# Layer 2 of an attention and two-layer feed-forward kernel: two passes of four slice pairs for three passes, smaller token blocks, another order of products

## The chip, the cores and the metric

One core of one Trainium2 chip runs the whole program: TensorE (PE) for matrix products, VectorE (DVE), ScalarE (ACT) and GpSimd (POOL) for elementwise work, SyncE (SP) as the queue that issues every DMA. The metric is device time in microseconds. The kernel before takes 1144.64 us (median of 3 runs, 1144.38 to 1147.03).

## What is computed

```python
attn_out = attention(q, k, v, tau)           # 4 batches x 8 heads x 576 x 64, thresholded softmax
x  = attn_out as (2304 tokens, 512)
h  = x @ w_in                                # layer 1: 512 -> 2048 -> 512
g  = where(h >= 1, h, where(h <= -1, 0, (h + 1) ** 2 / 4))
x  = g @ w_out
h2 = x @ w_in2                               # layer 2: 512 -> 2048 -> 512
out = (s * relu(h2) ** 2 + b) @ w_out2
```

The weights come as 64-bit floats and are converted on the chip. Every operand of a product is split in a high and a low part (a cast, and a subtraction that leaves the rest), and a product is three matmuls: high x high, high x low, low x high.

## The kernel before

Three stages follow each other: attention, with a part of layer 1 beside it (to about 440 us), the rest of layer 1 (to 702 us), and layer 2 (to the end).

**A planner sets the order.** The code records tasks with `add(alternatives, priority, reads, writes)`. An alternative is an engine with a time that the planner takes it to need. `Sched.run` then plays a list schedule and emits all instructions in that order, one fixed sequence for each engine. Where a task has several alternatives, `best` takes the engine that would end first; for tasks recorded before the point `sch.soft` a third of DVE's speed is assumed (`PENALTY`), later ones see its plain time. Banks of PSUM are taken by `Group`: the first free of the eight. Banks 0 and 1 are the two halves of one tile (`ps2_0` in the program), banks 2 and 3 of another (`ps2_1`), banks 4 to 7 are tiles of their own.

**Layer 1, late part.** `hidden` makes a tile of h (12 matmuls of 256 or 320 columns), which passes DVE, ACT, DVE, ACT, and a subtraction (`both_sub`, line 954, by DVE or POOL). `l1_out` multiplies it by w_out, three tiles behind (`LEAD`). `load_parts` brings a token block of x to a staging buffer by DMA and copies it into place with 4 x 2 copies (lines 916 to 918). Beside this the weights of layer 2 are prepared (`weight_set`, `half_rows`, `store`): loaded as 64-bit words, converted by one ACT and four DVE steps, combined, split, and put in place for the first pass, or stored to DRAM (`wD`) for later ones.

**Layer 2.** The 16 slices of 128 hidden units are worked off in passes, `PASSES = (3, 3, 2)` pairs of slices, so each pass goes over all tokens in three blocks of 768: nine steps. A step is `gemm1`, then `gemm2`.

- `gemm1` computes a 2 x 2 block product with seven products instead of eight. For each product p in `ORDER` the x operand is made (up to two subtractions, line 1190, and a split, line 1191) into one of three buffers of a ring, and each of the `nj` pairs of slices then takes six matmuls (line 1207) of 384 columns. Products 1, 6, 7, 4 add up in one bank of each pair (`A`), 5 and 3 in another (`Bk`), 2 in one of its own. After each product the bank is copied (`copied`, line 1141) or added (`joined`, line 1145) to a row in SBUF, before the next product of that bank may write it.
- When both halves of a row are there, `activated` runs relu (ACT line 1162 or POOL line 1163), square (ACT line 1164), scale and bias (DVE line 1165 or POOL line 1166), and the split into `G`.
- `gemm2` multiplies the rows of G with w_out2 (line 1239): for each row, for each 128 tokens, three matmuls of 512 columns into one bank per 128 tokens. In the first pass the sums go to DRAM (`yD`), in later ones the earlier sums are read back and joined.

All units of weights for the next pass are stored to DRAM during one pass, with the kit of buffers `kits[1]`, and fetched into place as the last step of that pass frees the places.

Of the kernel before, what the change touches and what calls it, by code (L numbers as in the profile page):

```python
# [362 lines left out]
def attention_then_ffn(tc, qk, v, tau, w1, w2, s2, b2, out):  # L363
# [62 lines left out]
    wD = dp.tile([11 * sum(PASSES[1:]), 128, 512], F32, name="wd")  # L426
# [389 lines left out]
    def final():  # L816
        late["cm"].__exit__(None, None, None)
        xg.__exit__(None, None, None)
        late["cm"] = tc.tile_pool(name="final", bufs=1, side="right")
        q = late["cm"].__enter__()  # L820
        arena["PR"] = q.tile([128, PR_BYTES // 4], F32R, name="pr")
        arena["PF"] = q.tile([128, PF_BYTES // 4], F32, name="pf")
# [80 lines left out]
    xp_b, yp_b = [Buf("LG", O_XP + 5120 * i, 4 * TM) for i in range(2)], Buf("LG", 0, 4 * TM)  # L903

    def load_parts(q, xs):
# [3 lines left out]
        for x, t in enumerate((XH, XL)):  # L909
            add([("sp", DMA_ISSUE, lambda x=x: nc.sync.dma_start(out=xp_b[x](0, 4 * T).rearrange("p (k t) -> p k t", k=4),  # L910
                                                          in_=xT[x, :, t0:t0 + T].rearrange("(k p) t -> p k t", p=128)))],
                pr, r=["late"] + [("xT", q, p, x) for p in range(H // 2)], w=xp_b[x].keys(0, 4 * T), lag=128 * 16 * T)
            for j in range(4):
                c = slice(j * T, j * T + T)
                k = ("XH", "XL")[x]
                add([("act", act_ns(T), lambda c=c, t=t, x=x: nc.scalar.copy(out=t[xs][:, c], in_=xp_b[x](c.start, T))),
                     ("pool", pfast_ns(T), lambda c=c, t=t, x=x: nc.gpsimd.tensor_copy(out=t[xs][:, c], in_=xp_b[x](c.start, T))),
                     ("dve", fast_ns(T), lambda c=c, t=t, x=x: nc.vector.tensor_copy(out=t[xs][:, c], in_=xp_b[x](c.start, T)), True)],
                    pr, r=xp_b[x].keys(j * T, T), w=[(k, xs, j)])
# [141 lines left out]
    class Pass:  # L1061

        def __init__(self, n, f0, nj, first, slots):
            self.n, self.f0, self.nj, self.first = n, f0, nj, first
            self.unit = [Buf(*places[i], 512, F32R) for i in slots[:11 * nj]]

        def product(self, p, j):
            return ORDER.index(p) * self.nj + j
# [4 lines left out]
        def rows(self):  # L1073
            return [2 * j + 1 for j in range(self.nj)] + [2 * j for j in range(self.nj)]

        def store(self, kit, n, val, kv, to, prio):

            u = [o_b[turn("o", NO)] if self.n else self.unit[i] for i in to]
# [334 lines left out]
```

## Time and profile before

| what | us |
|---|---|
| median of 3 runs | 1144.64 |
| the profiled execution | 1146.08 |
| its span (first to last instruction) | 1144.2 |
| attention and the part of layer 1 beside it | 0 to 440 |
| layer 1, the rest | 440 to 701.9 |
| layer 2, pass 1 (3 pairs) | 701.9 to 858.5 |
| layer 2, pass 2 (3 pairs) | 858.5 to 1012.7 |
| layer 2, pass 3 (2 pairs) and the last output | 1012.7 to 1144.2 |

A row of the trace gives the time that an engine was busy in a stretch, or one group of instructions (line, engine, operation, what it writes and reads), or what ended the idle time before an instruction. Matmuls overlap: one of 512 columns is shown with some 0.39 us and the next starts 0.23 us later, so the spacing of the starts is what counts.

### The profile page before, as it was taken

The page shows a single profiled execution, that of the slowest core. Times are in us where ns is not written, and L with a number is a line of the kernel's source. Part 1 is how long each engine was busy: PE and PEld are TensorE (multiplying, and loading weights), DVE is VectorE, ACT ScalarE, POOL GpSimd, SP SyncE. Part 2 cuts the span into 40 slices and gives each one's busy share as a digit, 9 for nine tenths or more (in the row PEclk, how much of TensorE's full clock was granted, in tenths as well). Part 3 has the DMA queues.
Part 4 walks back from the last instruction along what each step waited for, and adds up shares of the span by engine and source line. Part 5 has one row for each costly group of instructions (what it writes and reads, how often), then busy time and mean ns, then how long its engine had stood idle before and what let it go on. Part 6 is the DMA issues. An engine that isn't in the chain of part 4 may idle for free.

```text
span 1144.2 us, 19743 instructions
## 1 busy us (share of the span) xinstructions
PE 1084.8 (95%) x6910; PEld 936.7 (82%) x6910; DVE 834.1 (73%) x1792; ACT 688.3 (60%) x1340; POOL 419.5 (37%) x600
## 2 busy tenths in 40 slices
PE   9899999999999999999999999899998999988787
PEld 6557777888988989999999999787878888767566
DVE  6999999687587755599995555879687886726454
ACT  6998889778788876455553333646545473513322
POOL 5666766787588452000210000312232220413312
PEclk9999999999999999999999999999999999999999
DMA  5546453543444311544553423273949576423321
GB/s 179 182 144 177 128 169 108 155 126 98 128 122 128 96 53 47 169 140 159 164 165 111 129 98 101 74 257 136 342 161 355 189 262 221 156 94 128 110 92 56
DMA packets 95714, 169.06 MB, mean 148 GB/s; under 512 B 9600, under 2 KB 42368, under 8 KB 95616
## 3 DMA queue, kind: packets, MB, share of 16 engines
q1 hardware_dynamic: 95616, 167.81, 45.4%
q8 instruction: 54, 0.88, 0.3%
q14 instruction: 44, 0.36, 0.1%
HBM read 120.33 MB, written 47.45 MB: 147 GB/s over the span
## 4 chain that ended last, share of the span: by engine, by line
PE 65%; DVE 18%; ACT 10%; issue 3%; DMA 1%; POOL 1%; DVEq 0%; ACTq 0%; POOLq 0%
PE ps L1239 15%; PE ps L1207 14%; PE ps L941 10%; PE ps L1017 8%; PE ps L974 6%; PE ps L728 4%; PE ps L690 3%; DVE p L634 3%; PE ps L580 3%; ACT p L669 2%; ACT e L629 2%; DVE lg L1145 2%; PE ps L571 2%; DVE stt L626 1%; ACT pt L682 1%
## 5 line engine op out<-in xcount | busy, mean ns | idle before, releaser
L1239 PE MATMUL ps<-lr,pr 128*128 128x512 f32 x756 | 178.9, 396 | 2.7 <-DVE lg L1145 1.6
L1239 PEld LDWEIGHTS ps<-lr,pr 128*128 128x128 f32 x756 | 141.2, 188 | 38.9 <-ACT lf L1164 2.1
L1207 PE MATMUL ps<-lr 128*128 128x384 f32 x720 | 138.3, 342 | 20.1 <-ACT lg L1141 9.6
L1207 PEld LDWEIGHTS ps<-lr 128*128 128x128 f32 x720 | 123.5, 188 | 34.1 <-ACT lg L1141 14.4
L941 PE MATMUL ps<-xh,lr 128*128 128x256 f32 (+1 forms) x640 | 140.0, 299 | 1.8 <-DVE lf L951 1.7
L634 DVE SCALAR_TENSOR_TENSOR p<-ps,stt,e 128x576 f32<-128x576 f32 x144 | 116.0, 812 | 27.7 <-ACT e L629 16.5
L626 DVE TENSOR_REDUCE stt<-ps 128x1 f32<-128x576 f32 x144 | 105.9, 748 | 22.5 <-PE ps L580 12.7
L949 ACT ACTIVATE lf<-lf,cst 128x320 f32<-128x320 f32 (+1 forms) x128 | 68.8, 537 | 77.4 <-DVE lf L947 76.9
L629 ACT ACTIVATE e<-ps,stt 128x576 f32<-128x576 f32 x144 | 105.8, 748 | 14.6 <-DVE stt L626 11.7
L941 PEld LDWEIGHTS ps<-xh,lr 128*128 128x128 f32 x640 | 106.3, 188 | 4.8 <-DVE lf L951 2.7
L1141 ACT COPY lg<-ps 128x384 f32<-128x384 f32 x89 | 41.2, 482 | 114.6 <-PE ps L1207 114.2
L669 ACT ACTIVATE p<-p,stt 128x576 f32<-128x576 f32 (+3 forms) x106 | 86.4, 819 | 15.7 <-DVE stt L653 14.7
L941 PE MATMUL ps<-xl,lr 128*128 128x256 f32 (+1 forms) x320 | 94.1, 294 | 0.0
L974 PE MATMUL ps<-g,lr 128*128 128x320 f32 (+1 forms) x600 | 88.3, 299 | 0.5 <-ACT lf L983 0.5
L690 PE MATMUL ps<-ident,p 128*128 128x128 f32 x576 | 82.6, 275 | 3.8 <-ACT pt L682 2.2
L682 ACT COPY pt<-ps 128x512 f32<-128x512 f32 x141 | 79.4, 588 | 7.1 <-PE ps L690 6.5
L974 PEld LDWEIGHTS ps<-g,lr 128*128 128x128 f32 x600 | 81.9, 188 | 1.4 <-ACT lf L983 0.7
L953 ACT CAST g<-lf 128x320 fp32r<-128x320 f32 (+1 forms) x128 | 55.3, 432 | 45.4 <-DVE lf L951 44.4
L690 PEld LDWEIGHTS ps<-ident,p 128*128 128x128 f32 x576 | 66.4, 140 | 17.2 <-ACT pt L682 3.0
L1017 PE MATMUL ps<-g,wh 128*128 128x320 f32 (+1 forms) x384 | 78.7, 297 | 0.8 <-DVE lf L1027 0.6
L947 DVE TENSOR_SCALAR lf<-ps 128x320 f32<-128x320 f32 (+1 forms) x128 | 57.9, 453 | 28.7 <-PE ps L941 28.3
L951 DVE TENSOR_TENSOR lf<-lf,ps 128x320 f32<-128x320 f32 (+1 forms) x128 | 57.4, 449 | 26.0 <-ACT lf L949 24.5
(121 smaller groups left out, 2459.3 us busy)
## 6 DMA issues: line engine op xcount, KB each, us to landing
wd<-pr SPq DMA_DIRECT2D x55, 256.0 KB, 4.3
lg<-y1T SPq DMA_DIRECT2D x9, 1536.0 KB, 7.5
lg<-in_w_dram SPq DMA_DIRECT2D x23, 512.0 KB, 3.9
pf<-in_w_dram SPq DMA_DIRECT2D x21, 512.0 KB, 5.3
vr<-in_v_dram SPq DMA_DIRECT2D x32, 320.0 KB, 3.5
st<-in_w_dram SPq DMA_DIRECT2D x40, 256.0 KB, 3.8
lr<-wd SPq DMA_DIRECT2D x37, 256.0 KB, 5.8
r<-in_qk_dram SPq DMA_DIRECT2D x32, 288.0 KB, 3.1
```

Of the source, the lines that this page charges most:

```text
L626: add([("dve", 665, lambda: nc.vector.tensor_reduce(out=nm[:, x:x + 1], in_=Sv(), axis=AX.XY, op=ALU.min))], at(pr, "min"), r=[kg], w=[ks[ ...
L629: add([("act", 624, lambda: nc.scalar.activation(out=ev, in_=Sv(), func=AF.Exp, bias=nm[:, x:x + 1], scale=-1.0))], at(pr, "exp"), r=[kg, ...
L634: nc.vector.scalar_tensor_tensor(out=p[:, x * S:x * S + S].rearrange("p (a c) -> p a c", a=2), in0=Sv(), scalar=nthr[:, x:x + 1], in1=ev, ...
L669: nc.scalar.activation(out=p[i:j, o:o + w], in_=p[i:j, a:a + w], func=AF.Identity, scale=rc[i:j, x:x + 1], bias=un[i:j, x:x + 1])
L682: add([("act", actp_ns(n), lambda: [nc.scalar.copy(out=a, in_=b) for a, b in zip(dst, src())]), ("dve", dve_ns(n), lambda: [nc.vector.tens ...
L690: nc.tensor.transpose(bank[g.banks[0]][:, j * 128:(j + 1) * 128], p[:, c0 + j * 128:c0 + (j + 1) * 128], ident)
L941: nc.tensor.matmul(o, a, x, start=(n == 0), stop=(n == 11))
L949: add([("act", act_ns(T, True), lambda: nc.scalar.activation(out=c, in_=c, func=AF.Square, bias=half, scale=0.5))], fp, r=[], w=kc)
L974: nc.tensor.matmul(o, a[:, c], x, start=(f == 0 and n == 0), stop=(f == nf - 1 and n == 2))
L1017: nc.tensor.matmul(o, a[:, c], x, start=(f == f0 and n == 0), stop=(f == f1 - 1 and n == 2))
L1207: nc.tensor.matmul(o, a, y, start=(i == 0 and p in (1, 5, 2)), stop=(i == 5), skip_group_check=p not in (1, 5, 2))
L1239: nc.tensor.matmul(o, a, y, start=(f == rows[0] and s == 0), stop=(f == rows[-1] and s == 2))
```

## The change

Layer 2 runs in two passes of four pairs of slices. The tokens come in four blocks (640, 640, 512, 512), so there are eight steps, and a matmul of gemm1 has 320 or 256 columns. The order of the products is 1, 5, 6, 3, 7, 2, 4: neighbours write other banks, and the even rows are complete after product 2, the odd ones after product 4; gemm2 takes the even rows first. relu is on ACT alone. Layer 1's x goes by DMA straight into place. Of the first pass's 44 units of weights 12 have no place until layer 1 is over: they are stored to DRAM and fetched (`NPLACE`, `stored`). Two weight sets of the second pass are prepared early (`EARLY`). `sch.soft` is set behind the preparation of the first pass, so that DVE's penalty holds in the whole of layer 1. The planner's times for scale and bias are raised. There are 3 output buffers for the first pass (`y_b`) and 2 store buffers in kit 1 (`NO`), where there were 4 and 3. `PAD` moves the tiles `pr` and `pf` from an address of 32 modulo 64 to one of 0.

```diff
-PASSES = (3, 3, 2)
+PASSES = (4, 4)
-BT = 768
-HT = BT // 2
-ORDER = (1, 6, 7, 4, 5, 3, 2)
+BLOCKS = ((0, 640), (640, 640), (1280, 512), (1792, 512))
+BT = 640
+ORDER = (1, 5, 6, 3, 7, 2, 4)
-NLEFT, NEXTRA = 31, 10
+NLEFT, NPLACE = 32, 44
+EARLY = 2
...
-            add([("sp", DMA_ISSUE, lambda x=x: nc.sync.dma_start(out=xp_b[x](0, 4 * T).rearrange("p (k t) -> p k t", k=4),
...
-            for j in range(4):
...
-                add([("act", act_ns(T), lambda c=c, t=t, x=x: nc.scalar.copy(out=t[xs][:, c], in_=xp_b[x](c.start, T))),
...
+            add([("sp", DMA_ISSUE, lambda x=x, t=t: nc.sync.dma_start(out=t[xs][:, 0:4 * T].bitcast(F32).rearrange("p (k t) -> p k t", k=4),
...
+            self.unit = unit[:11 * nj]
+            self.stored = [bool(n) or u.mem == "PR" for u in self.unit]
...
         def rows(self):
-            return [2 * j + 1 for j in range(self.nj)] + [2 * j for j in range(self.nj)]
+            return [2 * j for j in range(self.nj)] + [2 * j + 1 for j in range(self.nj)]
...
-        add([("act", act_ns(n), lambda: nc.scalar.activation(out=h(), in_=h(), func=AF.Relu)),
-             ("pool", pfast_ns(n), lambda: nc.gpsimd.tensor_scalar(out=h(), in0=h(), scalar1=0.0, scalar2=0.0, op0=ALU.max, op1=ALU.add))], pr, w=kh)
+        add([("act", act_ns(n), lambda: nc.scalar.activation(out=h(), in_=h(), func=AF.Relu))], pr, w=kh)
...
-        made = {6: [(T1, b12, b11), (T2, b22, T1)], 7: [(b12, b22, b12)], 4: [(T2, b21, T2)]}
+        made = {5: [(T1, b12, b11)], 6: [(T2, b22, T1)], 7: [(b12, b22, b12)], 4: [(T2, b21, T2)]}
...
-                if p == 5:
-                    activated(t, G_b[2 * j + 1], po)
-                elif p == 2:
-                    activated(t, G_b[2 * j], po)
+                if p == 2:
+                    activated(T, even, G_b[2 * j], po)
+                elif p == 4:
+                    activated(T, odd, G_b[2 * j + 1], po)
...
-    sch.soft = len(sch.tasks)
...
+    for job in passes[0].jobs() + work[:EARLY]:
+        job(kits[0])
+    sch.soft = len(sch.tasks)
+    load_x(*BLOCKS[0])
+    for i, s in enumerate(passes[0].stored):
+        if s:
+            passes[0].fetch(i, fresh()[1])
```

What PE runs in gemm1 of the last step, before: 14 products of six matmuls, all of them on the two banks of the tile `ps2_0`, most behind a wait for ACT (`Activation_49`) or DVE.

```order
L1207 MATMUL ps2_0_89<-lr_66 128x384 [waits DVE_49,Pool_49]
L1207 MATMUL ps2_0_89<-lr_66 128x384 x11
L1207 MATMUL ps2_0_89<-lr_66 128x384 [waits Activation_49]
L1207 MATMUL ps2_0_89<-lr_66 128x384 x5
L1207 MATMUL ps2_0_89<-lr_66 128x384 [waits Activation_49]
L1207 MATMUL ps2_0_89<-lr_66 128x384 x5
```

And in the second step of the change: products 1 and 5 (four pairs each) and the start of 6.

```order
L1204 MATMUL ps2_0_89<-lr_66 128x320 [waits DVE_49,Pool_49]
L1204 MATMUL ps2_0_89<-lr_66 128x320 x11
L1204 MATMUL ps2_1_90<-lr_66 128x320 [waits Activation_49]
L1204 MATMUL ps2_1_90<-lr_66 128x320 x5
L1204 MATMUL ps1_1_92<-lr_66 128x320 x6
L1204 MATMUL ps2_1_90<-lr_66 128x320 [waits DVE_49,Pool_49]
L1204 MATMUL ps2_1_90<-lr_66 128x320 x5
L1204 MATMUL ps1_0_91<-lr_66 128x320 [waits Activation_49]
L1204 MATMUL ps1_0_91<-lr_66 128x320 x5
L1204 MATMUL ps4_0_1152<-lr_66 128x320 x6
L1204 MATMUL ps4_1_1153<-lr_66 128x320 x6
L1204 MATMUL ps2_0_89<-lr_66 128x320 x12
```

Seven other products now stand between two that add to one bank; `ps2_1` holds a bank of product 1 and one of product 5.

What DVE runs in layer 1's late part, before, in its full stretch: the two steps of a hidden tile, the conversions of weights (L885, L887) and the subtractions of both (L550 into `g` and `wl`).

```order
L951 TENSOR_TENSOR lf_67<-lf_67,ps1_1_92 128x256
L947 TENSOR_SCALAR lf_67<-ps1_0_91 128x256
L885 SCALAR_TENSOR_TENSOR lg_5309<-lg_5309 128x512
L550 TENSOR_TENSOR g5_80<-lf_67,g5_80 128x256
L951 TENSOR_TENSOR lf_67<-lf_67,ps1_0_91 128x256
L887 SCALAR_TENSOR_TENSOR lg_5309<-lg_5309 128x512
L550 TENSOR_TENSOR g0_75<-lf_67,g0_75 128x256
```

What POOL runs in the change there, where layer 2's first weight sets are made:

```order
L551 TENSOR_TENSOR g3_78<-lf_67,g3_78 128x256
L551 TENSOR_TENSOR lr_66<-lg_5309,lr_66 128x256 x2
L551 TENSOR_TENSOR g4_79<-lf_67,g4_79 128x256
L551 TENSOR_TENSOR lg_5309<-lg_5309 128x256
L551 TENSOR_TENSOR lr_66<-lg_5309,lr_66 128x256
L551 TENSOR_TENSOR g5_80<-lf_67,g5_80 128x256
L551 TENSOR_TENSOR lg_5309<-lg_5309 128x256 x3
```

The subtractions of the hidden tiles and of the weight sets have moved from DVE to POOL.

## Rows read from the trace of the kernel before

**Rows 1.** The page, part 1: busy us (share) xinstructions.

```profile
PE 1084.8 (95%) x6910; PEld 936.7 (82%) x6910; DVE 834.1 (73%) x1792; ACT 688.3 (60%) x1340; POOL 419.5 (37%) x600
```

**Rows 2.** Busy by stretch: layer 1's rest (sum), pass 3, layer 2 (sum).

```profile
sum 262.00, PE 261.14 PEld 256.54 DVE 189.90 ACT 125.18 POOL 18.30; mean PE 87.05 PEld 85.51 DVE 63.30 ACT 41.73 POOL 6.10
...
1012.70:1144.20 131.50, 103.84 (x469) 82.60 (x467) 64.89 (x85) 38.87 (x58) 33.13 (x23) 1.00 0.29 99
sum 442.30, PE 397.72 PEld 333.49 DVE 291.38 ACT 195.22 POOL 110.91; mean PE 132.57 PEld 111.16 DVE 97.13 ACT 65.07 POOL 36.97
```

**Rows 3.** L1207 by step: PE busy (x), PEld, clock, DMA; sums of 6, of 3.

```profile
858.50:885.10 26.60, 23.28 (x126) 21.51 (x125) 1.00 1.01 367
...
sum 158.60, PE 141.78 PEld 128.96; mean PE 23.63 PEld 21.49
...
sum 74.70, PE 52.54 PEld 41.92; mean PE 17.51 PEld 13.97
```

**Rows 4.** L1239 by step: the last of nine, and their sum.

```profile
1122.40:1139.80 17.40, 16.97 (x72) 13.26 (x72) 1.00 0.06 22
sum 204.60, PE 202.95 PEld 160.36; mean PE 22.55 PEld 17.82
```

**Rows 5.** Timeline of PE, unbroken runs: start, us, line, columns, count.

```profile
871.92 3.97 PE L1207 MATMUL ps<-lr 128*128 128x384 f32 x22
...
885.65 23.73 PE L1239 MATMUL ps<-lr,pr 128*128 128x512 f32 x101
...
290.20 3.97 PE L974 MATMUL ps<-g,lr 128*128 128x320 f32 x26
...
207.75 3.23 PE L974 MATMUL ps<-g,lr 128*128 128x256 f32 x26
```

**Rows 6.** Timeline of PE in a step of pass 3; [idle before <- releaser].

```profile
1054.95 2.27 PE L1207 MATMUL ps<-lr 128*128 128x384 f32 x12
1057.79 1.32 PE L1207 MATMUL ps<-lr 128*128 128x384 f32 x6 [0.57 <-ACT lg L1141]
...
1078.79 1.31 PE L1207 MATMUL ps<-lr,pr 128*128 128x384 f32 x6 [0.65 <-DVE lg L1145]
```

**Rows 7.** ACT at the same place.

```profile
1057.25 0.48 ACT L1141 COPY lg<-ps 128x384 f32<-128x384 f32 x1 [7.90 <-PE ps L1207]
```

**Rows 8.** Timeline of PE in the last step of pass 2.

```profile
981.84 2.32 PE L1207 MATMUL ps<-lr 128*128 128x384 f32 x12 [0.16 <-DVE lg L1145]
984.81 1.32 PE L1207 MATMUL ps<-lr 128*128 128x384 f32 x6 [0.65 <-DVE lg L1145]
986.86 2.31 PE L1239 MATMUL ps<-lr,pr 128*128 128x512 f32 x8 [0.74 <-DVE lg L1145]
```

**Rows 9.** Groups by line, layer 2: xcount | busy us, mean ns | idle before.

```profile
L1163 POOL TENSOR_SCALAR lg<-lg 128x768 f32<-128x768 f32 x17 | 47.5, 2800 | 26.4 <-DVE lg L1145 26.3
L550 DVE TENSOR_TENSOR pr<-lg,pr 128x768 fp32r<-128x768 f32 x47 | 46.3, 985 | 8.2 <-ACT pr L844 8.2
...
L1145 DVE TENSOR_TENSOR lg<-lg,ps 128x384 f32<-128x384 f32 x72 | 38.3, 551 | 36.5 <-PE ps L1207 36.1 <-PE ps L1239 0.2
...
L1165 DVE TENSOR_SCALAR lg<-lf,cst 128x768 f32<-128x768 f32 x35 | 27.3, 779 | 1.6 <-ACT lf L1164 1.6
...
L1162 ACT ACTIVATE lg<-lg 128x768 f32<-128x768 f32 x31 | 25.5, 841 | 35.2 <-DVE lg L1145 35.2
```

**Rows 10.** Groups by line and form: POOL, whole program; DVE in layer 1.

```profile
L549 POOL TENSOR_TENSOR g<-lf,g 128x320 fp32r<-128x320 f32 x27 | 23.7, 883 | 6.4 <-ACT g L953 5.8
L549 POOL TENSOR_TENSOR g<-lf,g 128x256 fp32r<-128x256 f32 x23 | 17.2, 748 | 2.0 <-ACT g L953 1.7
...
L880 POOL TENSOR_SCALAR lg<-lg 128x512 f32<-128x512 f32 x2 | 1.4, 710 | 15.5 <-ACT lg L877 15.5
...
L887 DVE SCALAR_TENSOR_TENSOR lg<-lg 128x512 uint32<-128x512 uint32 x23 | 15.9, 693 | 0.0
```

**Rows 11.** The page, part 6: fetch of a weight unit, us to landing.

```profile
lr<-wd SPq DMA_DIRECT2D x37, 256.0 KB, 5.8
```

More of the change, by code (lines that the diff above doesn't have):

```diff
@@ L821, in final @@
         arena["PR"] = q.tile([128, PR_BYTES // 4], F32R, name="pr")
-        arena["PF"] = q.tile([128, PF_BYTES // 4], F32, name="pf")
+        arena["PF"] = q.tile([128, (PF_BYTES + PAD) // 4], F32, name="pf")
     def after(tasks, fn, key, r=()):
@@ L901, in span @@
         return q // 2 * S + q % 2 * 256, 320 if q % 2 else 256
[L903 removed]
+    yp_b = Buf("LG", 0, 4 * TM)
     def load_parts(q, xs):
@@ L1061, in attention_then_ffn, with __init__ @@
     class Pass:
-        def __init__(self, n, f0, nj, first, slots):
-            self.n, self.f0, self.nj, self.first = n, f0, nj, first
-            self.unit = [Buf(*places[i], 512, F32R) for i in slots[:11 * nj]]
+        def __init__(self, n, f0, nj, first):
+            self.n, self.f0, self.nj, self.first, self.last = n, f0, nj, first, n + 1 == len(PASSES)
+            self.unit = unit[:11 * nj]
+            self.stored = [bool(n) or u.mem == "PR" for u in self.unit]
         def product(self, p, j):
-            return ORDER.index(p) * self.nj + j
+            return 7 * j + ORDER.index(p) if not self.n else ORDER.index(p) * self.nj + j
         def out(self, f, y):
@@ L1149, in product @@
         add([("pe", ns, mm, "r")], pr, r=r, w=[("bank", g), "pe order"], group=g)
-    def load_x(blk):
-        t0 = blk * BT
-        keys = [("y1", q, dm) for q in range(2 * B) for dm in range(4) if span(q)[0] < t0 + BT and sum(span(q)) > t0]
-        add([("sp", DMA_ISSUE, lambda: nc.sync.dma_start(out=x_b().rearrange("p (k t) -> p k t", k=4),
-                                                  in_=y1T[:, t0:t0 + BT].rearrange("(k p) t -> p k t", p=128)))],
-            fresh()[1], r=keys, w=x_b.keys(), lag=128 * 16 * BT)
@@ L1257, in gemm2 @@
             (joined if P.n else copied)(g, n, y, y.keys(), po)
-            add([("sp", DMA_ISSUE, lambda y=y, i=i: nc.sync.dma_start(out=(out if last else yD)[tokens(i), :], in_=y()))], po,
-                r=y.keys(), w=[] if last else [("yd", blk, i)], lag=128 * 4 * n)
+            add([("sp", DMA_ISSUE, lambda y=y, i=i: nc.sync.dma_start(out=(out if P.last else yD)[tokens(i), :], in_=y()))], po,
+                r=y.keys(), w=[] if P.last else [("yd", t0, i)], lag=128 * 4 * n)
             sums(i + ny)
@@ L1310, in attention_then_ffn @@
     after(layer1, final, "final")
[L1312 to L1327 removed]
+    passes = [Pass(n, 2 * sum(PASSES[:n]), nj, 11 * sum(PASSES[:n])) for n, nj in enumerate(PASSES)]
+    work = passes[1].jobs()
+    for job in passes[0].jobs() + work[:EARLY]:
[5 more added lines that the diff above has]
+            passes[0].fetch(i, fresh()[1])
+    steps = [(P, b) for P in passes for b in BLOCKS]
+    for k, (P, (t0, T)) in enumerate(steps):
+        if not t0:
             if P.n:
@@ L1330, in attention_then_ffn @@
                     P.fetch(i, fresh()[1])
-            if P.n + 1 < len(passes):
-                passes[P.n + 1].prepare(kits[1])
-        gemm1(P)
+            else:
+                for job in work[EARLY:]:
+                    job(kits[1])
+        gemm1(P, T)
         if k + 1 < len(steps):
-            load_x(steps[k + 1][1])
-        gemm2(P, blk, P.n == len(passes) - 1)
+            load_x(*steps[k + 1][1])
+        gemm2(P, t0, T)
     def fill(b):
```

137 lines of the change are left out of this document (60 added, 77 removed).

## The prediction

> **What bounds the kernel now.** I read the shares of the engines first, then the busy time by stretch, then PE's timeline in single steps. PE is busy 95% of the span [rows 1], but that holds for two different things. In the rest of layer 1 it has 261.14 of 262.0 us [rows 2]: nothing that other engines are relieved of can bring more than a microsecond there. In layer 2 a busy share misleads, since matmuls overlap, so I count pure time from the spacing of starts in unbroken runs [rows 5]. A run's length less the last matmul's own time (0.34, 0.39, 0.31, 0.28 us), divided by the number of gaps: (3.97 - 0.34) / 21 = 0.173 us for 384 columns, (23.73 - 0.39) / 100 = 0.233 for 512, (3.97 - 0.31) / 25 = 0.146 for 320, (3.23 - 0.28) / 25 = 0.118 for 256.
>
> gemm1 has 6 x 126 + 3 x 84 = 1008 matmuls, pure 174.4 us, and takes 158.6 + 74.7 = 233.3 [rows 3]. So it loses 58.9: the six steps with three pairs lose 158.6 - 756 x 0.173 = 27.8 (4.6 each), the three steps of pass 3 lose 74.7 - 252 x 0.173 = 31.1 (10.4 each). gemm2 has 864 matmuls, pure 201.3, takes 204.6 and loses 3.3 [rows 4]. Losses 62.2, and 4.4 us from the last product to the end (1144.2 - 1139.8) [rows 4]: 174.4 + 201.3 + 62.2 + 4.4 = 442.3, which is layer 2 [rows 2].
>
> Where the losses sit: in pass 3 nearly every group of six matmuls waits 0.57 to 0.65 us for ACT's copy or DVE's add of a bank [rows 6]. The copy of the first pair begins at 1057.25 [rows 7], just when the twelve matmuls of both pairs have ended (1057.22), and PE goes on at 1057.79 [rows 6], 0.06 after it: the two banks are halves of one tile, and the copy of one half is held until the write of the other is over. In the best step with three pairs the waits are few and stand at the end, for DVE's adds: 0.16 before product 2, 0.65 within it, 0.74 at the passage to gemm2 [rows 8].
>
> **The change, part by part.** The sum is made against the profiled execution, 1146.1 us; the median of the runs is 1.4 below it.
>
> *Matmul sizes.* gemm1 keeps its columns, in 672 matmuls of 320 and 672 of 256: 672 x (0.146 + 0.118) = 177.4 us for 174.4 [rows 5], **+3.0**. gemm2 keeps its 864. The Trainium skill (TensorE: Matmul & The Clock Gate, Back-to-back issue gap) gives N/2.4 + 2.5 ns for an isolated matmul, by which 336 more matmuls would cost 0.8 us; the rows, with some 13 ns beyond N/2.4, decide against it here.
>
> *Four pairs, and the new order.* This is the large term. Between two products that use one bank there now stands at least one product on other banks, of 4 x 6 x 0.146 = 3.5 us (640 tokens) or 2.8 us (512). A copy or add of 0.55 us and its hand-off [rows 9] fits in several times over. The 31.1 us of pass 3 have no place any more, nor have the waits of product 3 for the adds of 5 right before it. What stays is seen in the order: `ps2_1` still holds one bank of the first and one of the second sum in most steps, so a pair's product has one other product (0.88 or 0.71 us) to hide a copy or add of 0.46 or 0.37 (0.551 scaled by columns) and two hand-offs; that fits while ACT or DVE are free, and fails by up to one instruction of some 0.8 us when they are not. Product 2's third and fourth pair wait for the add of its first and second.
>
> The passage to gemm2: its first row is complete after product 2 of the first pair, and has three pairs and the whole of product 4 as cover, 7 x 0.88 = 6.2 us or 7 x 0.71 = 5.0. Its chain is one add (0.46), relu, square and cast on ACT (0.841 x 640/768 = 0.70 each), scale on DVE (0.65), subtraction (0.82) [rows 9] and six hand-offs, put at 0.1 each after the 0.06 above: 4.6 us, and 3.8 with 512. Alone it fits; the next rows' relus on ACT stand between, so I expect 0 to 1 us.
>
> Bounds for a step's loss: below, 0.9 us, if only gemm2's 0.4 a step (3.3 / 9) and a few hand-offs are left; above, 5.0, if steps lose as those with three pairs do now (4.6 + 0.4). I take the best of those steps, 25.5 - 126 x 0.173 = 3.7, without the quarter of it that the order removes, and with the final waits scaled by the smaller blocks (0.75): 1.3 + 1.1 = 2.4 for gemm1, 0.35 for gemm2, **2.75**, since its waits are those that stay [rows 8]. Eight steps: 22.0 (7 to 40) for 62.2: **-40.2**.
>
> *One pass less.* The x side (seven splits, four subtractions a block) is done twice instead of three times. On DVE this is 11 subtractions in three blocks, of 0.985 us by the nearest row [rows 9], some 32 us; also 18 adds of earlier sums go. DVE has 291 of 442 us in layer 2 [rows 2], so alone this brings nothing at the end; it is why queues are short where I assumed free engines.
>
> *relu on ACT alone.* 17 relus on POOL take 2.8 us each, for 0.84 on ACT [rows 9]. ACT has 195 of 442 us [rows 2], so it takes them; what they delay is part of the losses already counted. 0.
>
> *x of layer 1 into place.* The copies go from ACT, DVE and POOL, which are not the bound (PE 261.14 of 262.0 [rows 2]). The DMA must wait until the block before last is done with its buffer, and has then a block of six or more hidden tiles, some 19 us, while a transfer of similar kind takes 5.8 us [rows 11]. 0; without that cover each of six blocks would stand up to 6 us.
>
> *Subtractions on POOL (`sch.soft`).* In the change's order POOL has in layer 1's rest 107 subtractions of 256 columns (0.75), 37 of 320 (0.88), 20 of 512 (1.3 by the slope of the two) and 32 clamps (0.71) [rows 10]: 80 + 33 + 26 + 23 = 162 of 262 us. In the densest stretch, 18 hidden tiles, it is some 50 of 58 us. PE is three tiles ahead (9.5 us, at 24 matmuls of 0.118 to 0.146 each), so I put **+1** for short waits, 0 to 8.
>
> *Handover to layer 2.* The first product takes the bank that layer 1 leaves last, and four x subtractions stand before that eviction on DVE: **+0.6** (0 to 1.5). The 12 fetched units are first needed after a whole gemm1 and two rows of gemm2, over 30 us; 3.1 MB at the 367 GB/s that a step has seen [rows 3] take 9. 0.
>
> *Fetches between the passes.* 44 units are 11.5 MB, 31 us at 367 GB/s. Units come free all through the fourth step (42 us) and are used one after another through the next. 0; see the rivals.
>
> *Output buffers, store buffers, alignment.* Fewer buffers bring waits on DMA landings at two passages of the first pass; inside the 3.5 us of product 1. For `PAD` no row tells what the old address cost; DVE's 47 writes of 0.985 us to that tile [rows 9] run beside PE's products, so I put 0, and some tenths a step either way are inside the bounds of 0.9 and 5.0.
>
> Sum: +3.0 - 40.2 + 1 + 0.6 = **-35.6**, so 1146.1 - 35.6 = 1110.5 for the profiled execution and about 1109 for the median; I say **1110**.
>
> **The rivals.**
>
> *The waits stay.* Each step loses 5.0, as steps with three pairs do: 40 instead of 22, so 1128. For it: the planner's times are too short in places (relu on POOL: 2.8 us for the 0.88 that it assumes), and a pair's time shrinks with the block while hand-offs don't. Against it: the waits in [rows 8] are on adds that the new order moves apart.
>
> *Layer 1 becomes bound by POOL.* If POOL's subtractions and DVE's two-input conversions (0.69 each [rows 10], some twenty in the dense stretch, 14 us) can't run at once, that stretch holds 50 + 14 = 64 us of work in 58, and the weights' other subtractions queue behind. The lead of 9.5 us covers most; what is left I price at up to 8 us, 7 more than in the sum: 1117. For it: the stretch is dense without any lock. Against it: the subtractions are short (0.75), and PE needs a tile only after the lead; with 18.3 us of POOL in layer 1 [rows 2] the trace of before can't tell. The Trainium skill (SBUF — State Buffer, the section on its two separate sides) says that a DVE instruction with two SBUF inputs and a GpSimd instruction that reads SBUF lock each other out of a shared port pair for the whole instruction; by that rule this rival is the likelier, and no row here shows it alone.
>
> *The fetch is late.* If stores and x halve the rate, the 28 units of products take 40 us for the 22 of a gemm2; used one by one over another 20, some 8 us stay: 1118. In the trace of before the same passage has a full DMA share and a step of 26.6 us [rows 3], where the mean of the six is 26.4.
>
> *Slower: shared tiles chain the products.* If the tie between two halves of a tile holds more often than the order shows, products wait as in pass 3: 31.1 us over 42 groups, 0.74 us each. The gain without losses is 62.2 - 3.0 - 1.6 - 8 x 0.35 = 54.8, so it is gone at 74 waits of the 224 groups, more than nine of the 28 in a step. At 14 a step, all those on the two double tiles, it is 83 - 54.8 = +28: 1173. Against it: the order shows two to four products of a step that follow a use of the same tile at a distance of one, the others have three or more between.
>
> **How the numbers follow.** The forecast's mechanism has 0.70 (1097 to 1123), better than 1097 0.04, waits that stay 0.10 (half of it beyond 1127), POOL in layer 1 0.06, late fetch 0.05, chained products 0.05. From 1097 to 1127 is left out 0.04 + 0.05 + 0.05 = 0.14. A measurement of this kernel can tell some 0.3% (3.4 us) from no change. Of the chained products 0.03 end slower than that and 0.02 within; all else is faster: 0.95.
>
> **What would show it.** Layer 2 begins at 702 to 705 us and takes 402 to 420 us for 442.3. gemm1 takes about 24.5 + 2.4 us in steps of 640 tokens (168 x 0.146) and 19.8 + 2.4 in steps of 512. No run of groups of six with a wait before each is left; what waits there are stands at products 2, at 3 or 5, and at the passage to gemm2. relu has no POOL row, and the sums in PE rows are 672 + 672 + 864. Wrong would be: a step that loses over 5 us, layer 1 that ends after 708, or a first gemm1 of the second pass that waits for DMA.

## The result, and the profile after

The changed kernel takes **1091.21 us** (1091.0 to 1091.4, 4 runs) against 1144.51 (1144.16 to 1147.03): ratio 0.953, 95% interval 0.9513 to 0.9546, a gain of 53.3 us. The forecast was 1110 with a range down to 1097, and 0.04 for anything better: the sign and the mechanism held, the size did not. The profiled executions differ by 55.0 us (1146.08 and 1091.09).

First the page (shares of the engines), then the two late stretches [rows 1, 2]; columns as there.

```profile
PE 1065.4 (98%) x7246; PEld 943.0 (87%) x7246; DVE 751.8 (69%) x1632; ACT 687.2 (63%) x1398; POOL 505.0 (46%) x738
...
440.00:699.20 259.20, 258.46 (x1946) 254.39 (x1944) 162.81 (x295) 130.02 (x277) 173.47 (x200) 1.00 0.53 175
699.20:1089.20 390.00, 380.38 (x2208) 340.96 (x2208) 236.04 (x420) 188.40 (x359) 41.73 (x51) 1.00 0.39 134
```

Layer 2 takes 390.0 us for 442.3, and POOL has 173 us in layer 1's rest for 18. Now gemm1 by step (blocks of 640, 640, 512, 512; first pass, then second), with the sum of each pass, and the sum of gemm2's eight steps [rows 3, 4]:

```profile
699.20:726.50 27.30, 25.51 (x168) 24.64 (x168) 1.00 0.63 227
753.70:780.00 26.30, 25.29 (x168) 24.53 (x168) 1.00 0.56 195
807.80:829.90 22.10, 21.05 (x168) 20.27 (x168) 1.00 0.75 252
852.10:872.50 20.40, 20.39 (x168) 20.28 (x168) 1.00 0.99 346
sum 96.10, PE 92.24 PEld 89.73; mean PE 23.06 PEld 22.43
...
895.00:919.70 24.70, 24.70 (x168) 24.58 (x168) 1.00 0.47 154
947.00:971.70 24.70, 24.68 (x168) 24.53 (x167) 1.00 0.43 145
999.40:1019.60 20.20, 20.18 (x168) 20.16 (x167) 1.00 0.53 178
1042.10:1062.40 20.30, 20.30 (x168) 20.22 (x168) 1.00 0.18 65
sum 89.90, PE 89.87 PEld 89.49; mean PE 22.47 PEld 22.37
...
sum 199.00, PE 197.91 PEld 160.32; mean PE 24.74 PEld 20.04
```

In the second pass PE is busy for the whole of gemm1: nothing is lost there. The first pass loses 96.1 - 89.8 = 6.3 us (89.8 is four undisturbed steps, 2 x 24.7 + 2 x 20.2); in the first step alone 27.3 - 24.7 = 2.6. 96.1 + 89.9 + 199.0 + 5.0 (from the last product to the end, 1084.2 to 1089.2) = 390.0.

Next the spacing, from PE's timeline in gemm2, after:

```profile
926.62 20.56 PE L1232 MATMUL ps<-pr 128*128 128x512 f32 x90
...
1062.37 5.63 PE L1232 MATMUL ps<-lr,pr 128*128 128x512 f32 x24
```

(20.56 - 0.39) / 89 = 0.227 us and (5.63 - 0.39) / 23 = 0.228, for 0.233 before [rows 5]. The gaps found most often are 226 and 227 ns, 0.2267 us in the mean: 864 x 0.2267 = 195.9 us for the 201.3 of the forecast, 5.4 us that it did not have.

### The profile page after: what moved, and what is told of

Same layout as the page of the kernel before. It is cut to its first block, busy times and chain, and to the rows that moved or that the text cites. A ratio compares the mean times of both kernels' runs of the same rounds, so it can differ in the third digit from the quotient of the medians.

```text
span 1089.3 us, 20427 instructions
## 1 busy us (share of the span) xinstructions
PE 1065.4 (98%) x7246; PEld 943.0 (87%) x7246; DVE 751.8 (69%) x1632; ACT 687.2 (63%) x1398; POOL 505.0 (46%) x738
## 4 chain that ended last, share of the span: by engine, by line
PE 77%; ACT 10%; DVE 9%; issue 2%; POOL 1%; DMA 1%; DVEq 0%; ACTq 0%; POOLq 0%
PE ps L1232 18%; PE ps L1204 15%; PE ps L936 14%; PE ps L1012 10%; PE ps L969 6%; PE ps L730 4%; PE ps L692 3%; PE ps L582 3%; ACT p L671 3%; DVE p L636 3%; ACT e L631 2%; PE ps L573 2%; ACT pt L684 1%; DVE stt L628 1%; PE ps L731 1%
## 5 line engine op out<-in xcount | busy, mean ns | idle before, releaser
L1204 PE MATMUL ps<-lr 128*128 128x320 f32 (+1 forms) x1344 | 183.3, 297 | 3.7 <-DVE lg L1144 1.6
L1204 PEld LDWEIGHTS ps<-lr 128*128 128x128 f32 x1344 | 180.1, 190 | 7.4 <-issue 2.6
L1232 PE MATMUL ps<-pr 128*128 128x512 f32 x648 | 148.2, 389 | 0.0
L551 POOL TENSOR_TENSOR g<-lf,g 128x320 fp32r<-128x320 f32 (+1 forms) x128 | 110.7, 866 | 74.2 <-ACT g L948 71.8
L1232 PEld LDWEIGHTS ps<-pr 128*128 128x128 f32 x648 | 121.6, 188 | 25.2
L847 POOL CAST lr<-lg 128x512 fp32r<-128x512 f32 (+2 forms) x30 | 21.3, 709 | 229.6 <-PE ps L1204 181.4
L628 DVE TENSOR_REDUCE stt<-ps 128x1 f32<-128x576 f32 x144 | 105.8, 748 | 21.8 <-PE ps L582 12.9
L1140 ACT COPY lg<-ps 128x320 f32<-128x320 f32 (+2 forms) x115 | 44.2, 408 | 82.7 <-PE ps L1204 73.2
```

The source lines that it names most:

```text
L551: return [("pool", pool_ns(n), lambda: nc.gpsimd.tensor_tensor(out=o(), in0=x(), in1=y(), op=op)), ("dve", dve_ns(n), lambda: nc.vector.te ...
L628: add([("dve", 665, lambda: nc.vector.tensor_reduce(out=nm[:, x:x + 1], in_=Sv(), axis=AX.XY, op=ALU.min))], at(pr, "min"), r=[kg], w=[ks[ ...
L1204: nc.tensor.matmul(o, a, y, start=(i == 0 and p in (1, 5, 2)), stop=(i == 5), skip_group_check=p not in (1, 5, 2))
L1232: nc.tensor.matmul(o, a, y, start=(f == rows[0] and s == 0), stop=(f == rows[-1] and s == 2))
```

## The experiments

**The order, or the fourth pair?** Three runs, each with one of the two undone or done alone. In `old_order` the change has the products and rows in the order of before (the main lines of the edit):

```diff
-ORDER = (1, 5, 6, 3, 7, 2, 4)
+ORDER = (1, 6, 7, 4, 5, 3, 2)
...
-            return [2 * j for j in range(self.nj)] + [2 * j + 1 for j in range(self.nj)]
+            return [2 * j + 1 for j in range(self.nj)] + [2 * j for j in range(self.nj)]
...
```

> The changed kernel with one part undone: the products stand in the order of before (1, 6, 7, 4, 5, 3, 2), the odd rows come first; two passes of four pairs and blocks of 640 and 512 tokens stay. Theory A (the losses of gemm1 went because uses of one bank stand further apart, and the order and the fourth pair each give a part): three products of 0.88 or 0.71 us stand between two uses of a bank, for seven in the change and two of 1.04 us before; a step loses about 2 us where the change loses 0.1 to 2.6: some 1102 to 1110 us. Rival B (the fourth pair alone did it, the order brings nothing): 1091 to 1094. Rival C (the order alone did it): a step loses the 4.6 us of the steps of before, 8 x 4.6 = 37 for the change's 6: about 1122.

Measured: 1101.5 us (ratio to before 0.961, 0.959 to 0.963), layer 2 in 399.4 us for the change's 390.0: theory A, its size a little too large. `three_new_order` makes the opposite edit in the kernel before.

> The kernel before with one part of the change: the order of products 1, 5, 6, 3, 7, 2, 4 and the even rows first; three passes (3, 3, 2) and blocks of 768 tokens stay. Theory A: five products of 1.04 us stand between two uses of a bank in passes 1 and 2, three in pass 3; the 62 us lost in layer 2 fall to 10 to 25, so 1092 to 1107. Rival B (the order brings nothing without the fourth pair): 1140 to 1145. Rival C (the order alone did it): as much as the change, 1091 to 1096, since pure matmul time is 3 us less in this form.

Measured: 1116.4 (0.974, 0.972 to 0.976), layer 2 in 411.0, a miss of theory A's 1092 to 1107. `three_small_blocks` makes three passes out of the change's two:

```diff
-PASSES = (4, 4)
+PASSES = (3, 3, 2)
...
```

> The changed kernel with one part undone: three passes of 3, 3 and 2 pairs for two of 4; the new order, the blocks of 640 and 512 tokens, relu on ACT and the alignment stay (so twelve steps, with as many matmuls of the same sizes in all). Theory A (a pass of fewer pairs loses time because fewer products stand between the last add of a row and its use in gemm2, five with three pairs and three with two, and the products are shorter in these blocks): eight steps lose 2 to 3 us, the four of the last pass 4 to 5: 32 to 44 us of losses for some 10 in the change: 1113 to 1125. Rival (not the number of pairs but the smaller blocks brought the gain, since each step's chains are shorter): 1100 or less.

Measured: 1114.4 (0.972, 0.971 to 0.974), layer 2 in 413.6. So neither does it alone, and smaller blocks without the fourth pair bring little: 1114.4 for 1116.4. (Four pairs with blocks of 768 were not run.) By the ratios the order alone brings 2.6%, the pairs and all the rest without it 3.9%, both 4.7%: less than the sum, so they remove some of the same losses. In `three_new_order` PE's waits inside gemm1 nearly go, as theory A said (3.5 us by the same view, for 36 before), but the chain from a row's last add to gemm2, which it does not name, no longer fits; the theory of `three_small_blocks` names this place, and its range holds. First `three_new_order`: PE's timeline at the passage to gemm2 in pass 3, and PE's main waits in layer 2 (us in total, times, longest). Then the same passage in the last pass of `three_small_blocks`.

```profile
1053.13 0.73 PE L1239 MATMUL ps<-pr 128*128 128x512 f32 x2 [2.25 <-ACT pr L844]
1054.40 5.55 PE L1239 MATMUL ps<-pr 128*128 128x512 f32 x16 [0.54 <-DVE pr L550]
...
PE ps L1239 <- ACT pr L844: 10.1, 6, 2.2
PE ps L1239 <- DVE pr L550: 5.6, 8, 1.1
```

```profile
1045.33 2.87 PE L1232 MATMUL ps<-lr,pr 128*128 128x512 f32 x7 [2.23 <-ACT pr L846]
```

With two pairs only three products stand between the first even row's last add and gemm2 (3 x 1.04 = 3.1 us of cover, 0.173 x 6 each). With four there are seven.

Such a wait can cost more than its own length. Behind the one at 1053 us the 16 matmuls of the second row above take 5.55 us, where the same 16 of the step before take 3.92. The difference is TensorE's granted clock: 0.50 (the lower of its two levels, 1.2 GHz) in the first stretch below, 1.00 in the second, although a wait of 2.25 us stood ahead of both.

```profile
1056.00:1058.00 2.00, 2.00 (x6) 1.63 (x5) 2.00 (x3) 1.39 (x2) 0.00 (x0) 0.50 0.00 0
1018.50:1023.50 5.00, 4.46 (x18) 3.41 (x19) 5.00 (x7) 3.84 (x5) 2.49 (x1) 1.00 0.12 43
...
1019.77 3.92 PE L1239 MATMUL ps<-pr 128*128 128x512 f32 x16 [0.54 <-DVE pr L550]
```

The clock falls twice in layer 2 of `three_new_order` and four times in that of `three_small_blocks`; at 5.55 - 3.92 = 1.6 us each that is an estimated 3 and 6.5 us of what they lose against the change. Before, in the change and in `old_order` it is 1.00 all through layer 2, so it has no part in the gain.

In `old_order` about half of PE's waits in layer 2 (6.1 of 11.9 us) stand in the last product, 2, each ahead of one or two pairs (six matmuls a pair) and each for an add that frees a bank; another 3.3 us stand in gemm2, for the same kind of add. PE's timeline in its last step:

```profile
1070.71 0.98 PE L1204 MATMUL ps<-lr 128*128 128x256 f32 x6 [0.75 <-DVE lg L1144]
1072.20 0.98 PE L1204 MATMUL ps<-lr 128*128 128x256 f32 x6 [0.51 <-DVE lg L1144]
```

**The smaller spacing in gemm2.** `old_align` has PAD 256 for 288 in the change; `before_align` is the kernel before with

```diff
-        arena["PF"] = q.tile([128, PF_BYTES // 4], F32, name="pf")
+        arena["PF"] = q.tile([128, (PF_BYTES + 32) // 4], F32, name="pf")
```

> The changed kernel with one part undone: PAD is 256 for 288, so that the tiles pr and pf stand again at 32 modulo 64 bytes. In gemm2 of the change matmuls of 512 columns start every 0.227 us, in the kernel before every 0.232 to 0.235, except 99 whose both operands lie in pr (0.227 too). Theory H (PE is slower where the two operands stand at different offsets modulo 64): the 216 matmuls of gemm2 that read lr and pr lose 0.006 us each, 1.3 us in all: 1092 to 1093. Rival H2 (every matmul that reads pr at the old address is slower): 864 x 0.006 = 5.2, so 1096. Rival as in the prediction (alignment does nothing; the smaller spacing has another cause): 1091.

> The kernel before with one part of the change: 32 bytes of padding behind pf, so that pr and pf stand at 0 modulo 64 bytes. Theory H: the 756 matmuls of gemm2 that read lr and pr start every 0.227 us for 0.233, 4.5 us in all: 1139 to 1140.5 by the fast runs of before at 1144.5. Rival H2: 864 of them, 5.2 us: 1139. Rival (alignment does nothing): 1144 to 1146, spacing as before.

Measured: 1092.7 (1092.2 to 1093.1) for 1091.2, and 1141.9 for the 1146.1 of before beside it (ratio 0.997, 0.996 to 0.998). The times are near the limit of what can be told; the timelines decide. PE in gemm2, first `old_align`, then `before_align`:

```profile
1064.13 5.75 PE L1232 MATMUL ps<-lr,pr 128*128 128x512 f32 x24
1069.72 16.49 PE L1232 MATMUL ps<-pr 128*128 128x512 f32 x72
```

```profile
882.04 24.76 PE L1239 MATMUL ps<-lr,pr 128*128 128x512 f32 x108 [0.45 <-ACT lg L1162]
```

With the old address the matmuls of `lr` and `pr` go back to (5.75 - 0.39) / 23 = 0.233, those of `pr` alone stay at (16.49 - 0.39) / 71 = 0.227. With the new one in the kernel before, `lr` and `pr` go at (24.76 - 0.39) / 107 = 0.228. H holds, H2 falls: `pr` at the old address is fast with itself. So of the 5.4 us that the forecast missed PAD brings only 1.3 (216 x 0.006; 1.5 between the medians). The other 4 come from the 648 of the 864 matmuls that read both operands from `pr`, where the w_out2 units lie: 108 did so before, and were already faster than the forecast had it, 540 are new. Only a shift by 32 bytes was run, so the rule for other addresses is open.

**What the first pass still loses.** `no_prep` leaves out the jobs and fetches of the second pass's weights; `dve_load` adds DVE work at the lowest priority, by the edit below. Each was run once.

```diff
+                if P.last and j < 3 and p in (1, 5, 6, 3, 7):
+                    o0, o1 = outs[1]
+                    add([("dve", fast_ns(512), lambda: nc.vector.tensor_tensor(out=o0(), in0=o0(dt=F32), in1=o1(dt=F32), op=ALU.add), True)],
+                        back(), r=o1.keys(), w=o0.keys())
```

> The changed kernel without the preparation of the second pass's weights in the first pass and without their fetches: the second pass works with the weights of the first, so that part of the result is left out. In the change the four steps of the first pass lose 2.6, 1.6, 1.9 and 0.3 us in gemm1, those of the second 0.0 to 0.2, and DVE is busy 35 to 42 of 54 us a step in the first three of them, 27 of 52 later. Theory A2 (what is left of the losses comes from the queue of DVE and ACT, lengthened by the preparation): the first pass loses 2 us or less in all, the time is 1086 to 1088. Rival (the losses of the first pass come from the end of layer 1 and from the order itself): 1090 to 1092.

> The changed kernel with work added for DVE in the second pass: 15 additions of 128x512 (about 0.69 us each by the nearest rows, 10 us a step) of two buffers that nobody reads, at the lowest priority, as the preparation of weights has it in the first pass. Theory A2 (the length of DVE's queue is what makes PE wait): the steps of the second pass lose 1 to 2 us each for 0.1 now: 1095 to 1099. Rival (the order leaves room enough for a busy DVE too; the first pass's waits have another cause): 1090 to 1092.

Measured: `no_prep` 1088.8; gemm1 of the first pass, in sum:

```profile
sum 93.40, PE 91.15 PEld 89.62; mean PE 22.79 PEld 22.41
```

So 2.7 of the 6.3 us are the preparation's, less than theory A2 asked: 3.6 stay, 2.6 of them in the first step, and their cause is open. `dve_load`: 1100.6, more than theory A2's 1095 to 1099. The planner did not spread the work: 58 of the 60 additions run between 852 and 930 us, most of them in two gemm1 steps, the last of the first pass and the first of the second. PE's timeline, then the busy times of three gemm1 steps (PE, PEld, DVE, ...), two loaded and one not:

```profile
871.42 7.47 PE L1204 MATMUL ps<-lr 128*128 128x256 f32 x48 [2.13 <-DVE lg L1144]
914.02 15.53 PE L1204 MATMUL ps<-lr 128*128 128x320 f32 x102 [2.83 <-DVE lg L1141]
...
852.30:878.70 26.40, 22.43 (x169) 21.84 (x168) 25.48 (x45) 10.57 (x25) 1.66 (x2) 0.94 0.97 335
901.30:929.40 28.10, 25.21 (x170) 24.69 (x170) 24.02 (x39) 11.31 (x23) 3.74 (x4) 1.00 0.42 134
956.70:981.40 24.70, 24.70 (x170) 24.68 (x169) 12.86 (x24) 10.21 (x22) 2.97 (x4) 1.00 0.43 145
```

With DVE at 25.5 of 26.4 and 24.0 of 28.1 us the steps lose 6.0 and 3.4 us (1.6 of the 6.0 by the granted clock, 0.94 in that step's mean); at 12.9 of 24.7 nothing. The cover holds while DVE has room, as theory A2 says, though two steps paid instead of four.

**relu on POOL again.** `relu_pool` gives relu its alternative on POOL back, and the planner its old times for scale and bias.

> The changed kernel with one part undone: relu may go to POOL again, and scale and bias have their old prices; some twenty relus of the 64 go to POOL, where one of 640 or 512 columns takes some 2.3 or 1.9 us (2.8 x columns / 768, from the trace of before). Theory A (the order leaves 5 to 6 us between the last add of a gemm2 row and its use, and the chain of 4.6 us grows by 1.6 where relu is on POOL): only first rows are late, 0 to 1 us a step, so 1091 to 1096. Rival (the relus on POOL were a main cause of the losses of before): 1100 or more.

Measured: 1094.0 (1093.6 to 1096.4), 2.8 more; layer 2 takes 392.5 us for 390.0. 25 relus went to POOL, and the loss stands where theory A has it, at rows that gemm2 needs, but in two waits (0.7 and 2.0 us) rather than in each step. Groups by form, then PE's longest wait:

```profile
L1161 POOL TENSOR_SCALAR lg<-lg 128x512 f32<-128x512 f32 x15 | 29.6, 1992 | 24.2 <-DVE lg L1144 24.2
L1161 POOL TENSOR_SCALAR lg<-lg 128x640 f32<-128x640 f32 x10 | 25.1, 2525 | 19.5 <-DVE lg L1144 18.0 <-ACT lg L1140 1.4
...
979.03 3.25 PE L1233 MATMUL ps<-lr,pr 128*128 128x512 f32 x13 [1.97 <-DVE pr L552]
```

**Layer 1: what the forecast put at nothing.** `staging` restores the eight copies of x and, to make room, the old kit; `small_kit` only the old kit:

```diff
-    kits = [kit_at("LG", O_KIT, 3, 4), kit_at("PF", O_KIT2, 2, 2)]
+    kits = [kit_at("LG", O_KIT, 2, 3), kit_at("PF", O_KIT2, 2, 2)]
```

> The changed kernel with one part undone: x of layer 1 goes through staging buffers and eight copies a token block again (and the first kit has 2 load and 3 work buffers again, to make room). Theory, as in the prediction (PE bounds the rest of layer 1, the copies lie beside it): 1090.5 to 1092.5, layer 1 ends within 1 us of the change's. Rival (ACT, DVE and POOL are near their limit in that stretch of the change, and six blocks of eight copies of some 0.5 us, 24 us, delay PE or the weight sets): 1094 or more.

> The changed kernel with the first kit of buffers as before (2 load and 3 work buffers for 3 and 4); x of layer 1 still goes by DMA into place. The run with staging had this kit too, was 20.8 us longer, and all of that stood in one wait of PE before layer 2: the last weight sets were stored at 706 to 715 us, for 669 in the change. Theory K (the smaller kit slows the conversion of the weights, so that the sets are late): 1105 to 1112. Rival C (the copies of x, on ACT, DVE and POOL ahead of the conversions, made the sets late): 1091 to 1094.

Measured: 1112.0 (1110.6 to 1112.8) and 1095.5 (1095.3 to 1097.9). A miss for the first, and neither theory for the second: the kit makes up 4 of the 21 us, the copies with it the other 16. Most of it is one wait of PE ahead of layer 2's first product. PE's timeline in `staging`, `small_kit`, and in `early4`, which prepares two more sets:

```profile
722.28 0.64 PE L1211 MATMUL ps<-lr 128*128 128x320 f32 x1 [18.82 <-ACT lr L846]
```

```profile
705.39 0.63 PE L1204 MATMUL ps<-lr 128*128 128x320 f32 x1 [5.82 <-ACT lr L846]
```

```profile
710.50 0.63 PE L1204 MATMUL ps<-lr 128*128 128x320 f32 x1 [9.81 <-ACT lr L846]
```

In `staging` and `small_kit` layer 2's first x had been loaded long before (657.40 and 616.50 us). What came late was the place for its split: the ring buffers in `lr` lie where the first kit keeps finished weights until they are stored. ACT's timeline in `staging`, the cast that makes the high part (the last stores stand at 714.91):

```profile
721.50 0.72 ACT L846 CAST lr<-lg 128x640 fp32r<-128x640 f32 x1 [12.35 <-DMA wd<-lr]
```

How much room the preparation has, the runs with EARLY 0, 3, 4 and 6 for 2 tell.

> The changed kernel with EARLY 4 for 2: all four weight sets of products of the second pass are prepared in layer 1, beside PE, and only the w_out2 units in the first pass. Without any preparation in the first pass the time was 2.4 us shorter. Theory A2 (DVE's queue in the first pass makes PE wait, and layer 1 has room: DVE 163, POOL 173, ACT 130 of 259 us): 1089.5 to 1090.7. Rival (layer 1 is full in the stretch where the sets are made, or its stores collide with the fetches before layer 2): 1092 or more.

> The changed kernel with EARLY 6: four weight sets and two of eight w_out2 rows of the second pass are prepared in layer 1. Theory A2: 1089 to 1090.5, at or below the run with 4. Rival (layer 1 has no room for more): above the run with 4 by 1 us or more.

> The changed kernel with EARLY 3 for 2. With 2 the last store of a weight set stands at 669 us and layer 2 begins at 699; with 4 the last stood at 703, and PE waited 10 us for x, which queues behind the stores; with 6, 22 us. Theory S (layer 1 has room for as many sets as end before its last tiles, one set takes some 15 to 17 us): the last store stands at 684 to 688, no wait is added, and the first pass saves a part of the 2.4 us that all preparation costs there: 1090 to 1091. Rival (the sets delay the fetches and x at once, with no such room): 1094 or more.

> The changed kernel with EARLY 0: all weight sets of the second pass are prepared in the first pass. Theory S (what the preparation costs in the first pass is DVE's queue): the first pass loses 1 to 3 us more than the 6 of the change: 1091.5 to 1094. Rival (the preparation beside gemm1 is covered whatever its size): 1090.5 to 1091.5.

Measured: 0: 1091.6; 2: 1091.2; 3: 1090.3 (1089.8 to 1090.7); 4: 1102.6; 6: 1113.8. Theory S holds for 3; for 0 the interval (1090.95 to 1091.66) does not separate it from its rival; A2's hope for 4 and 6 was wrong. With the larger kit layer 2's first x goes to a place under the kit's work buffers too, so its load is issued only when the last set has left them. That load (`lg<-y1T`) and the last stores in SP's timeline for EARLY 0, 3 and 4 (2: 668.64):

```profile
636.00 0.47 SPq L1152 DMA_DIRECT2D lg<-y1T  x1
636.52 0.61 SPq L1083 DMA_DIRECT2D wd<-lr  x1
```

```profile
686.11 0.37 SPq L1152 DMA_DIRECT2D lg<-y1T  x1
686.54 1.69 SPq L1083 DMA_DIRECT2D wd<-lr  x3
```

```profile
702.24 0.41 SPq L1152 DMA_DIRECT2D lg<-y1T  x1
702.70 0.55 SPq L1083 DMA_DIRECT2D wd<-lr  x1
```

Each set moves it by some 16 us. From the load to the first product it is 8.3 us (702.24 to 710.50), and layer 1 ends at some 700, so the load may stand as late as 691: the change has 22 us of room, and one more set still fits. With EARLY 6 the load stands at 702.25 too, but the last stores at 714.81, and the first product at 721.96: there the ring is what comes late again.

Why so little? `soft_old` puts most subtractions of layer 1 back to DVE; `soft_early4` and `soft_early6` do the same with EARLY 4 and 6.

```diff
     after(sch.tasks[:], switch, "late")
+    sch.soft = len(sch.tasks)
...
-    sch.soft = len(sch.tasks)
     load_x(*BLOCKS[0])
```

> The changed kernel with one part undone: the point sch.soft stands before the weights of layer 1's rest again, so that DVE, at its plain price, takes most subtractions of layer 1 and POOL few. Theory (as in the prediction: in the rest of layer 1 PE is the bound with either choice, and a lead of three tiles covers DVE or POOL): layer 1's end moves by less than 1.5 us, the time is 1090 to 1093. Rival (DVE has more weights to convert in this stretch than it had before, 32 conversions of 3 steps and eight and more sets, and can't take the subtractions too): layer 1 ends 4 us later or more, the time is 1095 or more.

> The run soft_old (subtractions of layer 1 mostly on DVE) with EARLY 4 for 2. In soft_old DVE had 204 of 261 us to do, and yet the last weight set was stored at 640 us for 669 in the change; its conversions took 0.74, 0.69 and 0.47 us for 1.05, 0.87 and 0.72 in the change, where POOL subtracts beside them. Theory L (POOL's subtractions lengthen DVE's conversions, so that sharing the work with POOL makes the preparation later, not earlier): two more sets end at 665 to 680, before layer 1 is over, no wait of 10 us stands before layer 2 as in early4, 1090 to 1093. Rival (DVE is then too full, and the sets or layer 1's tiles are late): 1097 or more.

> As before with EARLY 6, which with subtractions on POOL took 1113.8 us. Theory L: the last store stands at 680 to 700 us, the time is 1089.5 to 1095 (above 1092 if the last stores hold up the fetches). Rival (DVE too full): 1105 or more.

Measured: 1092.9 (1092.6 to 1093.2), 1091.4 (1091.0 to 1092.2) and 1092.1 (1091.8 to 1095.5). With EARLY 2 the choice of engine changes 1.7 us, in the range of `soft_old`'s theory. With 4 and 6 it decides, against 1102.6 and 1113.8 with the same sets and the subtractions on POOL: theory L's times hold. Its cause is shown only in part. DVE's conversions in layer 1's rest, by form (xcount | busy us, mean ns), in the change and in `soft_old`:

```profile
L887 DVE SCALAR_TENSOR_TENSOR lg<-lg 128x512 uint32<-128x512 uint32 x32 | 33.5, 1046 | 0.3
L889 DVE SCALAR_TENSOR_TENSOR lg<-lg 128x512 uint32<-128x512 uint32 x32 | 27.7, 866 | 0.1
L885 DVE TENSOR_SCALAR lg<-lg 128x512 uint32<-128x512 uint32 x32 | 22.7, 720 | 7.0 <-POOL lg L882 6.7
```

```profile
L887 DVE SCALAR_TENSOR_TENSOR lg<-lg 128x512 uint32<-128x512 uint32 x32 | 23.6, 741 | 0.1
L889 DVE SCALAR_TENSOR_TENSOR lg<-lg 128x512 uint32<-128x512 uint32 x32 | 21.9, 687 | 0.0
L885 DVE TENSOR_SCALAR lg<-lg 128x512 uint32<-128x512 uint32 x32 | 14.8, 467 | 0.0
```

DVE has 204 us to do there in `soft_old` for 163, and yet x is loaded at 638.9 for 668.6: with POOL subtracting beside it, a conversion's three steps take 2.63 us for 1.90. The Trainium skill (SBUF — State Buffer, Who interferes with whom) says that a DVE instruction contends with GpSimd when it has two SBUF inputs and the GpSimd instruction reads SBUF, or when it runs in a 2-port performance mode, which `tensor_scalar` can enter; the longer rows agree in direction, and no row here shows the mode of `L885`, the step with one input.

But longer conversions don't fill DVE. Busy times (PE, PEld, DVE, ACT, POOL) from 560 to 600 us, where the sets are made, in the change and in `soft_old`:

```profile
560.00:600.00 40.00, 40.00 (x295) 39.86 (x294) 22.54 (x44) 19.63 (x44) 36.48 (x47) 1.00 0.52 163
```

```profile
560.00:600.00 40.00, 39.71 (x287) 38.98 (x287) 36.22 (x79) 20.25 (x43) 11.11 (x14) 1.00 0.60 190
```

In the change POOL is busy 36.5 of 40 us and DVE 22.5. So POOL's own queue, in which a set's subtractions stand between those of layer 1, may hold up the preparation as much as DVE's longer steps do. The runs show that subtractions on POOL make the sets late; which of the two ways counts for how much stays open.

The best version found is `early3`, 1090.3; its interval to before (0.9501 to 0.9529) overlaps the change's.

## Why the prediction was right or wrong

The reading of the bound, the sign and the main mechanism were right: no groups of six with a wait each, gemm1 near its pure time. The forecast for the profiled execution was 1110.5, measured 1091.1, 19.4 less. By the terms:

- **Losses, 22.0 (8 x 2.75): measured 9.5** (gemm1 6.3 + 0.1; gemm2 199.0 - 195.9 = 3.1), 12.5 less. This is the step that failed most, and in it gemm1's part: 8 x 2.4 = 19.2 forecast, 6.4 measured, while gemm2's 8 x 0.35 = 2.8 was near. It scaled the best step of before (3.7) to 2.4, instead of pricing the waits of the new order one by one. The same part had the numbers for that: seven products of 0.71 to 0.88 us against a chain of 4.6 at the passage to gemm2, and 2.8 to 3.5 us against a copy or add of 0.55 between two uses of a bank. Where the cover was longer than the chain and DVE had room, as in the second pass, gemm1 lost next to nothing, not three quarters; a step there lost less than the 0.9 that was called the lower bound.
- **Alignment 0, gemm2 "keeps its 864": measured -5.4**, by the faster gemm2 (1.3 by PAD, 4 by the matmuls of `pr` alone). The rows gave one spacing for 512 columns [rows 5]; the faster matmuls of `pr` alone, there in the trace of before, were not looked for.
- **Matmul sizes, +3.0: measured +5.2** (2 x 89.8 = 179.6 for 174.4), since 0.146 and 0.118 are 0.147 and 0.120 in long runs.
- **Layer 1 and handover, +1.6: measured -0.8** (from the 3001st matmul to layer 2, 272.3 for 273.1 us). PE bound this stretch, as said, but the sum asked only whether PE waits inside it. The weights' preparation must clear the places of layer 2's first x and of its split before the stretch ends, x's some 8 us before, and `staging` shows what 0 for "x into place" hid: without that part and the larger kit that it makes room for, the change would be 20.8 us slower. The rival with POOL was right that its subtractions hold something up, and wrong in what: PE's tiles were covered by the lead, the preparation paid, out of its room.
- **relu, 0:** on POOL it would cost 2.8 (`relu_pool`). **Fetches, 0:** right; the step in which they run has a DMA share of 0.99 and loses nothing.
- **Not of the change: -1.9.** The 3001st matmul, in attention, starts at 427.0 for 428.8 us, where both kernels run the same code; over all runs here it lies between 427.0 and 428.8. What moves it stays open. It is about as much as the profiled execution of before lies above its median (1.6). The tail took 5.0 for 4.4, +0.6.

-12.5 - 5.4 + 2.2 - 2.4 - 1.9 + 0.6 = -19.4. Of the rivals, waits that stay came back only with DVE nearly full (`dve_load`), and chained products did not come: the second pass has no wait for a copy but one of 0.2 us. The fetch was not late.

## What to carry to other kernels

Price each wait of a new order by its own cover (products in between, times the spacing) and its own chain: a chain that fits cost nothing here, and a scaled old loss overstates it. A stretch bound by one engine still has a second deadline, the work that must be ready when it ends: find the last load and the last store of that work, the places that they hold, and their distance from the end before calling a part free. Before moving work to an idle engine ask how full its queue becomes and how long the instructions of both engines take beside each other. And where a wait of PE gets long, look at the granted clock behind it too.

## What the runs showed of the hardware

- Matmuls of 512 columns that read `lr` and `pr` start every 0.228 us, and every 0.233 when `pr` stands 32 bytes off (`old_align` and `before_align`, in both directions); those that read `pr` alone start every 0.227 at either address.
- DVE's 512-column conversions take 1046, 866 and 720 ns in the mean where most subtractions run on POOL, and 741, 687 and 467 where most run on DVE (the change and `soft_old`).
- POOL's in-place relu takes 1.99 us for 512 and 2.53 us for 640 columns, where ACT takes 0.63 and 0.73 (`relu_pool` and the change).
- After waits of PE of 2.25 us the granted clock stayed at 1.00 once and fell to 0.50 twice (`three_new_order`, 1018, 1053 and 1089 us); at 0.50 16 matmuls took 5.55 us for 3.92.
